# A transformer block on one Trainium2 core: the second half's eight normalised token tiles are turned on VectorE and through DRAM instead of on TensorE, and some background work is moved

## The chip, the cores and the metric

The kernel runs on one core of one Trainium2 chip. The core has four compute engines with queues of their own: PE (TensorE, matmuls), DVE (VectorE), ACT (ScalarE) and POOL (GpSimd), and SP (SyncE), which here only issues DMAs. Each queue is worked off in order. The metric is device microseconds of one execution; lower is better.

## The reference, cut to what matters

2048 tokens of width 576, all float32. The layer norm of x feeds two branches whose results are added to x:

```python
x  = A_x                                          # 1 x 2048 x 576
xn = (x - mean(x)) / sqrt(var(x) + 1e-5)
qkv = xn @ wqkv                                   # 576 x 1728; 32 heads of 18
# query s sees keys s, s-2, ..., s-14 (W = 8, dilation 2; places before 0 masked)
o   = softmax(q . k / sqrt(18)) . v
a   = o @ wo                                      # 576 x 576
h   = xn @ w1 + b1                                # 576 -> 4608
m   = (h * tanh(softplus(h))) @ w2                # Mish; 4608 -> 576
return x + a + m
```

## The kernel before, in words

**Tiling.** The tokens are worked on in two halves of 1024 (`hf` = 0, 1), each half as eight tiles of 128 tokens, four to a block `b` (0, 1). A float32 product is made of three matmul passes on fp32r values: every operand is split into a high part (a cast to fp32r, on ACT) and a low part (operand minus high part, a subtract on DVE or POOL). TensorE contracts over the partitions, so the normalised tokens must lie with the 576 features on the partitions: `XTs[hf, b]` holds them as four 128-feature slices plus a rest of 64, high parts and low parts, 512 tokens wide (the tile `xt_1_0` or `xt_1_1` for the second half).

**How the second half's tokens got there.** `x_load` (L105) fetches a tile of 128 tokens (`xn`), `norm1` (L139) normalises it on ACT, and POOL copies the last 64 features beside themselves (L140). `ln_transpose` copies a rest for block 1 on POOL (L192, L194) and calls `transpose_split`, which turns the tile by five matmuls against an identity (L75, L76), or six where a rest goes with it (L78), into PSUM; ACT casts the high parts out of PSUM (L81, L86) and DVE subtracts the low parts (L82, L87). Each of the eight tiles has a slot `("t", 1, b, jj)` of its own in the plan. Tiles 0 to 2 are turned between the last pieces of the first half's MLP; the other five between the second half's first qkv items.

**The MLP.** A unit `q` makes 256 hidden columns: `m1_part` runs 512-wide matmuls into PSUM banks `h` (L674, L680), `take` copies a bank (L708), DVE adds another bank (`c`, L719), ACT applies Mish (L720) and casts the high part (L725), POOL makes the low part (L726). `m2_pair` then multiplies by w2 in chunks `("p", 0, q, b, p)` of 24 matmuls of 288 columns (L774) into the four PSUM buffers `out`, and DVE adds each result to an accumulator (L778), four adds to a chunk. `q` = 17 is the last unit of the first half; its chunks come in the order (1,0), (1,1), (0,0), (0,1). In the second half most units go through a scheme of seven products to a pair of units: `u_sum` (L808), `u_high` (ACT) and `u_low` (L820) make the left operands, `p_item` multiplies (L866) and adds (L872) or copies (L870) into `accP` tiles, `p_join` (L875, POOL) joins those at the end, and `a_split` (L829) makes the plain operands of the units that follow (multiplied at L887). `y_store` (L1048) sends the first half's accumulators to DRAM.

**Attention** runs beside all this: POOL multiplies (L537, L575), DVE reduces (L542, L581), and each finished pair of heads is turned on DVE (`o_turn`, L597: a 32 x 32 block transpose of 128 x 576) and sent to DRAM by four DMAs of 72 KB (`o_send`, L606), whose access pattern completes the transpose.

**What sets the order.** `plan` is a list of slots; each has its main work and a list of background functions, put there by `before(slot, fn)`. The program is emitted slot by slot, and each engine's queue has its instructions in exactly that order. A slot is one piece of the PE's work (a chunk of 24 matmuls, a part of a unit, a qkv item), or empty. `soon` holds functions for the start of the next slot, `behind_adds` names slots whose attention sum is emitted at the slot's end. Every DMA signals one of eight completion semaphores (DMAHW0 to DMAHW7, called lanes below), taken in turn, and its queue first waits until the DMA that used that lane before has landed.

Of the kernel before, what the change touches and what calls it, by code (L numbers as in the profile page):

```python
# [8 lines left out]
F32 = mybir.dt.float32  # L9
# [8 lines left out]
P = 128  # L18
NH = 2
SH = S // NH  # L20
NB = 2
# [18 lines left out]
def block_kernel(ctx: ExitStack, tc: tile.TileContext, x, wq, wo, w1, b1, w2, mask, out):  # L40
# [26 lines left out]
    def transpose_split(src, dst, col, extra=None, pair=False):  # L67
        n = next(tpn)
        if pair:
            ta, tb = (ps.tile([P, 512], F32, tag="out", bufs=4, name=f"tt{k}_{n}") for k in range(2))  # L70
        else:
            ta = ps.tile([P, 512], F32, tag="h", bufs=4, name=f"ta_{n}")
            tb = ps.tile([P, 512], F32, tag="h", bufs=4, name=f"tb_{n}")
# [29 lines left out]
    def x_load(n):  # L103
        xn = sb.tile([P, 5 * P], F32, tag="xn", bufs=XNB, name=f"xn_1_{n}_{next(tpn)}")
        nc.sync.dma_start(xn[:, 0:D], x_tile(1, n))  # L105
        xns[1, n] = xn
# [30 lines left out]
    def norm1(n):  # L137
        xn = xns[1, n]
        nc.scalar.activation(xn[:, 0:D], xn[:, 0:D], AF.Identity, bias=nm1[:, n, :], scale=rs1[:, n, :])  # L139
        nc.gpsimd.tensor_copy(xn[:, D:D + 64], xn[:, KT * P:D])  # L140

    group = {}
# [41 lines left out]
    def ln_transpose(hf, b, jj):  # L184
# [10 lines left out]
        transpose_split(xn, XTs[hf, b], jj * P, rem if b else None, (hf, b) == (1, 0) and jj < 3)  # L195
# [314 lines left out]
    behind_adds, now = set(), [0]  # L510

    def attention(hf):
# [4 lines left out]
        def flush():  # L517
            if behind[0] is not None:
                if now[0] in behind_adds:
                    tail.append(behind[0])  # L520
                else:
                    behind[0]()
                behind[0] = None

        for pair in range(NQ * UQ // PU):
# [44 lines left out]
            for k, vt in enumerate(vs):  # L570
                for h in range(2):
# [8 lines left out]
                    def red(pr=pr, og=og, c0=k * CU + h * DH, last=(k, h) == (PU - 1, 1), pair=pair):  # L580
                        nc.vector.tensor_reduce(og[:, c0:c0 + DH, :].rearrange("p d j -> p j d"), pr, axis=AX,  # L581
                                                op=ALU.add)
                        if last:
                            soon.append(lambda: o_turn(hf, pair, og))
# [585 lines left out]
    def pr_(hf, q, b, p, alias=None):  # L1170
        def end():
            if hf == 0 and q == NP - 1:
                for jj in (2 * p, 2 * p + 1):
                    y_store(b * JB + jj)
        add(("p", hf, q, b, p), lambda: ((m2_cols if hf else m2_pair)(hf, q, b, p), end()), alias=alias)
# [56 lines left out]
    def tr(b, jj):  # L1232
        add(("t", 1, b, jj), lambda: ln_transpose(1, b, jj))
# [185 lines left out]
    for g, (e, k, s) in enumerate(items):  # L1419
        lead = items[g - 3][2] if g >= 3 else spot(1, 0, 5) + 2 * g  # L1420
        before(lead + 1, lambda e=e, k=k: p_fetch(e, k))
        for qq in range(2):
            ds = {(0, 0): (-6, -5, -5), (0, 1): (-2, -1, 0), (1, 0): (0, -4, -2), (1, 1): (0, -2, -2), (2, 0): (0, -3, -2), (2, 1): (0, -3, -2), (3, 0): (-4, -3, -2), (3, 1): (-4, -2, -1), (4, 0): (0, -3, -3), (4, 1): (0, -3, -2), (5, 0): (-1, -3, -3), (5, 1): (0, -3, -2), (6, 0): (-4, -3, -1), (6, 1): (-4, -3, -2)}[k, qq]
            if (e, k, qq) == (0, 0, 1):
                ds = (-2, -1, -1)
            if (e, k, qq) == (OC - 1, 0, 0):
                ds = (-5, -4, -4)
            for d, f in zip(ds[1:], (u_high, u_low)):
# [3 lines left out]
    J = 2 * OC + 1  # L1432
    for n, (a, b) in enumerate((("P6", "P1"), ("P7", "P6"), ("P6", "P5"), ("P2", "P1"), ("P3", "P6"), ("P4", "P7"), ("P5", "P7"))):
# [3 lines left out]
    for b in range(NB):  # L1437
        for j in range(2):
            before(spot(1, J, 0) + (2,3,1,2)[2 * b + j], lambda b=b, j=j: a_split(b, j))

# [32 lines left out]
    i = spot(0, NP - 2, 0)  # L1473
    for jj in range(JB):
        before(i + 2 * jj, lambda jj=jj: x_load(jj))
        before(i + 2 * jj + 6, lambda jj=jj: norm1(jj))
        before(at["t", 1, 0, jj] + 2, lambda jj=jj: x_load(JB + jj))
    for jj in range(JB):
        before(at["p", 0, NP - 1, 1, 1] + jj, lambda jj=jj: norm1(JB + jj))
# [6 lines left out]

    att = {}
    behind_adds.add((at["p", "x", OC - 1, 4]))
# [123 lines left out]
```

## Time and profile before

| | |
|---|---|
| time, median of 3 runs | 1113.11 us (1113.07 to 1113.46) |
| the profiled execution | 1113.54 us, span 1111.8 us, TensorE clock 1.000 |
| busy, share of the span | PE 99%, DVE 76%, ACT 45%, POOL 71% |
| DMA | 271.6 MB, mean 244 GB/s |

A row of the timeline reads: start in us from the span's start, time from its first start to its last end, engine, line, operation, out<-in, shape, and how many instructions in a row it stands for; in brackets the engine's idle time ahead of it and what ended it. PE matmuls overlap one another, so the time from one row's start to the next row's start, and not the duration, is what a row costs. A group row has the count, the total busy time and the mean duration of one.

### The profile page before, as it was taken

What the parts mean: (1) busy time and instruction counts of PE and PEld (TensorE: products, weight loads), DVE (VectorE), ACT (ScalarE), POOL (GpSimd) and SP (SyncE); (2) the same over time, 40 slices, a digit from 0 to 9 for tenths busy, and PEclk for the clock granted to TensorE, in tenths of its full rate; (3) what the DMA queues carried; (4) which work ended last, traced back from release to release, by engine and by line L of the source; (5) the groups of instructions that cost most, each with busy time, mean ns of one, the idle gap of its engine ahead of it and who ended that gap; (6) DMA issues with size and microseconds to landing.
All of it is one profiled execution on the core that took longest, in us unless ns stands there. A gap on an engine that the chain in (4) does not pass through costs nothing.

```text
span 1111.8 us, 18206 instructions
## 1 busy us (share of the span) xinstructions
PE 1103.0 (99%) x6550; PEld 1014.7 (91%) x6550; DVE 850.0 (76%) x1367; ACT 499.2 (45%) x917; POOL 790.6 (71%) x639
## 2 busy tenths in 40 slices
PE   8999999999999999999999999999999999999998
PEld 8999899999999999999999888989989999999998
DVE  6359788888889888897656577786876677777786
ACT  5544655544454544555333354433433344343353
POOL 2479777766679688685788667666688976867542
PEclk9999999999999999999999999999999999999999
DMA  6899696868777758675598798665674657776674
GB/s 202 283 312 313 229 347 223 283 235 275 259 243 264 266 210 300 248 253 202 188 328 257 228 378 297 217 198 197 222 223 169 210 195 216 244 286 220 181 232 141
DMA packets 178270, 271.60 MB, mean 244 GB/s; under 512 B 53218, under 2 KB 120068, under 8 KB 178180
## 3 DMA queue, kind: packets, MB, share of 16 engines
q1 hardware_dynamic: 178180, 270.44, 71.6%
q8 instruction: 52, 0.85, 0.3%
q14 instruction: 38, 0.31, 0.1%
HBM read 160.39 MB, written 110.00 MB: 243 GB/s over the span
## 4 chain that ended last, share of the span: by engine, by line
PE 86%; POOL 5%; DVE 4%; issue 2%; ACT 2%; DMA 2%; SPq 0%; POOLq 0%; DVEq 0%; ACTq 0%
PE h L674 27%; PE po L774 21%; PE po L887 11%; PE pq L348 9%; PE h L680 5%; PE o L1070 5%; PE po L866 4%; PE z L446 3%; POOL pv L575 1%; POOL s L624 1%; DMA accP<-in_x 1%; POOL accP L875 1%; DVE rm L808 1%; DVE accP L872 0%; DVE u L820 0%
## 5 line engine op out<-in xcount | busy, mean ns | idle before, releaser
L774 PEld LDWEIGHTS po<-w,act 128*128 128x128 f32 x1728 | 236.4, 188 | 6.0 <-POOL act L726 0.4
L774 PE MATMUL po<-w,act 128*128 128x288 f32 x1728 | 240.7, 295 | 0.2 <-POOL act L726 0.2
L537 POOL TENSOR_TENSOR pr<-q,kv 128x576 f32<-128x576 f32 x128 | 197.2, 1566 | 8.0 <-DMA q<-q_d 4.9
L726 POOL TENSOR_TENSOR act<-c,act 128x512 fp32r<-128x512 f32 x81 | 107.4, 1326 | 128.3 <-ACT act L725 128.3
L575 POOL TENSOR_TENSOR pv<-L,kv 128x576 f32<-128x576 f32 x128 | 177.8, 1484 | 26.2 <-DVE L L568 21.2
L778 DVE TENSOR_TENSOR acc<-po,acc 128x288 f32<-128x288 f32 x288 | 119.5, 449 | 29.9 <-PE po L774 28.8
L348 PE MATMUL pq<-wq,xt 128*128 128x432 f32 x672 | 136.4, 361 | 1.0 <-ACT xt L81 1.0
L887 PEld LDWEIGHTS po<-w,act 128*128 128x128 f32 x960 | 130.8, 188 | 4.5 <-POOL act L829 1.2
L887 PE MATMUL po<-w,act 128*128 128x288 f32 x960 | 133.4, 295 | 1.0 <-POOL act L829 1.0
L348 PEld LDWEIGHTS pq<-wq,xt 128*128 128x128 f32 x672 | 125.0, 188 | 8.0 <-ACT xt L81 1.6
L720 ACT ACTIVATE c<-c,b1c 128x512 f32<-128x512 f32 x81 | 58.7, 725 | 140.5 <-DVE c L719 140.3
L674 PE MATMUL h<-xt,t 128*128 128x512 f32 x432 | 110.6, 391 | 0.2 <-DVE c L719 0.2
L674 PE MATMUL h<-S,t 128*128 128x512 f32 x432 | 110.7, 391 | 0.0
L542 DVE TENSOR_REDUCE L<-pr 128x64 f32<-128x1152 f32 x64 | 85.8, 1342 | 26.3 <-POOL pr L537 26.2
L581 DVE TENSOR_REDUCE og<-pv 128x144 f32<-128x1152 f32 x64 | 86.0, 1346 | 25.7 <-POOL pv L575 25.6
L674 PE MATMUL h<-xt,wa 128*128 128x512 f32 x432 | 104.1, 390 | 0.0
L708 ACT COPY c<-h 128x512 f32<-128x512 f32 x81 | 47.4, 586 | 124.8 <-PE h L680 73.8
L866 PEld LDWEIGHTS po<-pw,u 128*128 128x128 f32 x672 | 92.0, 188 | 5.3 <-issue 0.9
L674 PEld LDWEIGHTS h<-xt,wa 128*128 128x128 f32 x432 | 80.9, 188 | 17.0
L866 PE MATMUL po<-pw,u 128*128 128x288 f32 x672 | 94.7, 296 | 1.3 <-issue 0.5
L674 PEld LDWEIGHTS h<-xt,t 128*128 128x128 f32 x432 | 79.1, 188 | 15.2 <-DVE c L719 0.5
L890 DVE TENSOR_TENSOR accP<-po,accP 128x288 f32<-128x288 f32 x160 | 68.8, 453 | 29.1 <-PE po L887 27.5
(228 smaller groups left out, 1854.2 us busy)
## 6 DMA issues: line engine op xcount, KB each, us to landing
kv<-kv_d SPq DMA_DIRECT2D x64, 396.0 KB, 5.0
kept_t<-t SPq DMA_DIRECT2D x36, 512.0 KB, 4.6
t<-kept_t SPq DMA_DIRECT2D x36, 512.0 KB, 6.4
rw<-in_w SPq DMA_DIRECT2D x36, 320.0 KB, 4.6
kept_wa<-wa SPq DMA_DIRECT2D x18, 640.0 KB, 4.7
kept_w<-w SPq DMA_DIRECT2D x20, 576.0 KB, 3.7
wa<-kept_wa SPq DMA_DIRECT2D x18, 640.0 KB, 4.8
w<-kept_w SPq DMA_DIRECT2D x20, 576.0 KB, 4.2
```

What stands on the lines that cost most here:

```text
L348: nc.tensor.matmul(pq[:, 0:432], XT[:, xi, tok], wt[wi][:, hl, 0:432], start=i == 0, stop=i == len(seq) - 1)
L537: nc.gpsimd.tensor_tensor(out=pr[:, x:x + hh], in0=q[:, j0 + x:j0 + x + hh, None, :].to_broadcast([P, hh, W, CU]), in1=win(kt, 0, CU, j0 + ...
L542: nc.vector.tensor_reduce(L[:, k, j0:j0 + hj].rearrange("p j w h -> p (j w h)"), pr.rearrange("p j w (h d) -> p (j w h) d", h=2), axis=AX, ...
L575: nc.gpsimd.tensor_tensor(out=pr[:, x:x + hj].rearrange("p j d w -> p j w d"), in0=L[:, k, x:x + hj, :, h:h + 1].to_broadcast([P, hj, W, DH]),
L581: nc.vector.tensor_reduce(og[:, c0:c0 + DH, :].rearrange("p d j -> p j d"), pr, axis=AX, op=ALU.add)
L674: nc.tensor.matmul(ph, wt[:, wl, wk * P:(wk + 1) * P], X[:, xs, :], start=first and i == 0, stop=last and i == len(seq) - 1, skip_group_ch ...
L726: nc.gpsimd.tensor_tensor(out=a[:, 1, :], in0=t, in1=a[:, 0, :].bitcast(F32), op=ALU.subtract)
L774: nc.tensor.matmul(po, acts[hf, q, b, j][:, al, tok], done["w2", hf, 2 * q + j][:, wl, c * HC:(c + 1) * HC], start=i == 0, stop=i == 5)
L778: nc.vector.tensor_tensor(out=t, in0=po, in1=t, op=ALU.add)
L866: nc.tensor.matmul(po, units[e, k, qq][:, al, tok], w[:, qq, wl, :], start=i == 0, stop=i == 5)
L887: nc.tensor.matmul(po, acts[hf, q, b, j][:, al, tok], done["w2", hf, 2 * q + j][:, wl, c * HC:(c + 1) * HC], start=i == 0, stop=i == 5)
L890: nc.vector.tensor_tensor(out=t, in0=po, in1=t, op=ALU.add)
```

## The change

For the second half only, the turn of the eight tiles leaves TensorE.

- **Taken out:** `ln_transpose(1, ...)`, that is 44 matmuls of 128 x 128 (four tiles of five, four of six), their PSUM tiles, the ACT casts and DVE subtracts that read these, and POOL's eight copies at L140. The slots `("t", 1, b, jj)` stay, empty.
- **Put in, per tile:** the load, now 3 or 6 slots before the turn (in a `raw` buffer for tiles 4 to 7), `norm1` one slot before the turn, `x_turn` (after's L143, a DVE block transpose of 128 x 576 into `xT_a` or `xT_b` in turns), `x_put` (L152: four DMAs of 72 KB, issued on ACT's queue, one in each of the four slots after the turn, to a DRAM tile `xT_d`), `x_back` (L156, L159: three DMAs on SP's queue, 256 KB and two of 32 KB, into an `xn` buffer, features now on the partitions), `x_high` (the casts on ACT, L180, and POOL's rest, as before) and one slot later `x_low` (the subtracts on DVE, L185), both now reading SBUF.
- **When:** with e the slot `("t", 1, 0, 3)`, which stands ahead of the first half's last chunks, the turns are at e-22, e-19, e-16, e-13, e-9, e-6, e-3 and e; the casts at e, e+2, e+4, e+6 (block 0) and e+7, e+9, e+11, e+13 (block 1).
- **Moved beside that:** `a_split` goes ahead of the `p_join`s of its slot; the low part of the operand S3's second unit (`u_low`, k = 0) comes one slot earlier for every pair of units; for the first pair, two sums come at other slots; three attention pieces are emitted later in or after their slot (`behind_adds`, `behind_next`, `o_turn`); `y_store` comes two slots after its chunk instead of at the chunk's end.

```diff
+    def x_turn(n):
+        if n == 0:
+            xTs["a"] = sb.tile([P, D], F32, tag="acc", bufs=9, name="xT_a")
+            xTs["b"] = sb.tile([P, 2 * 432], F32, tag="r3", bufs=1, name="xT_b")[:, 0:D]
+        t = xTs["ab"[n % 2]]
+        nc.vector.transpose(t, xns[1, n][:, 0:D])
+        xTs[n] = t
+
+    def x_put(n, g):
+        t = xTs[n]
+        if g == 0:
+            xT_d[n] = dram.tile([D, P], F32, name=f"xT_d{n}")
+        rows = xT_d[n].rearrange("(n i) p -> i n p", i=32)
+        part = slice(g * 32, (g + 1) * 32)
+        nc.scalar.dma_start(rows[:, :, part], t[part].rearrange("i (n k) -> i n k", k=32))
+
+    def x_back(n):
+        xn = xns[1, n] = sb.tile([P, 5 * P], F32, tag="xn", bufs=XNB, name=f"xn_t_{n}")
+        nc.sync.dma_start(xn[:, 0:KT * P].rearrange("p (k t) -> p k t", k=KT),
+                          xT_d[n][0:KT * P].rearrange("(k p) t -> p k t", p=P))
+        for r_ in range(2):
+            nc.sync.dma_start(xn[r_ * 64:(r_ + 1) * 64, KT * P:], xT_d[n][KT * P:D])
...
+    def x_high(n):
...
+        if b == 0:
+            nc.gpsimd.tensor_copy(rem, xr)
+        else:
+            nc.gpsimd.tensor_tensor(out=rem, in0=rem, in1=xr, op=ALU.subtract)
+        for s_, hi, lo in x_parts(n):
+            nc.scalar.copy(hi, s_)
+
+    def x_low(n):
+        for k, (s_, hi, lo) in enumerate(x_parts(n)):
+            r_ = slice(64 if k else 0, P)
+            nc.vector.tensor_tensor(out=lo[r_], in0=s_[r_], in1=hi[r_].bitcast(F32), op=ALU.subtract)
...
-        add(("t", 1, b, jj), lambda: ln_transpose(1, b, jj))
+        add(("t", 1, b, jj))
...
+    i, e = spot(0, NP - 3, 8), at["t", 1, 0, JB - 1]
+    for n in range(TJ):
+        b_, jj = divmod(n, JB)
+        turn = e - 9 + 3 * jj if b_ else i + 3 * jj + 3
+        split = e + (7, 9, 11, 13)[jj] if b_ else e + 2 * jj
+        before(turn - (6 if b_ else 3), lambda n=n: x_load(n, "raw" if n >= JB else "xn"))
+        before(turn - 1, lambda n=n: norm1(n))
+        before(turn, lambda n=n: x_turn(n))
+        for g in range(4):
+            before(turn + 1 + g, lambda n=n, g=g: x_put(n, g))
+        before(e + 2 + 2 * jj if b_ else split - 6, lambda n=n: x_back(n))
+        before(split, lambda n=n: x_high(n))
+        before(split + 1, lambda n=n: x_low(n))
...
-    behind_adds.add((at["p", "x", OC - 1, 4]))
+    behind_adds.update((at["p", "x", OC - 1, 4], at["p", "x", 0, 4]))
+    behind_next.add(at["m", 1, 10, 3])
```

Three places in the queues. First DVE's queue at e, before. `c21` is the last `c` add of `q` = 17; `tt0`, `tt1`, `ta` and `tb` are PSUM tiles with turned tokens; the first row after the gap is an attention sum, and the adds to `acc_0_1_0` take the results of chunk (1,0):

```order
L82 TENSOR_TENSOR xt_1_0_6052<-tt0_50_6129,xt_1_0_6052 128x4x128
L87 TENSOR_TENSOR xt_1_0_6052<-tt1_50_6130,xt_1_0_6052 64x128
L719 TENSOR_TENSOR c21_0_17_6008<-h3_0_17_5954,c21_0_17_6008 128x512
...
L581 TENSOR_REDUCE og_0_5_6120<-pv_0_5_0_0_6121 128x8x18
L82 TENSOR_TENSOR xt_1_0_6052<-tt0_52_6198,xt_1_0_6052 128x4x128
L87 TENSOR_TENSOR xt_1_0_6052<-tt1_52_6199,xt_1_0_6052 64x128
L82 TENSOR_TENSOR xt_1_0_6052<-ta_54_6227,xt_1_0_6052 128x4x128
L87 TENSOR_TENSOR xt_1_0_6052<-tb_54_6228,xt_1_0_6052 64x128
L778 TENSOR_TENSOR acc_0_1_0_183<-po_0_17_1_0_0_6240,acc_0_1_0_183 128x288
L778 TENSOR_TENSOR acc_0_1_0_183<-po_0_17_1_0_1_6248,acc_0_1_0_183 128x288
```

and in the changed kernel (`xT_a`, `xT_b`: the turned tiles 6 and 7 on their way to DRAM; `xn_t_0`: tile 0 come back):

```order
L143 STREAM_TRANSPOSE xT_a_5679<-xn_1_6_50_6047 128x576
L771 TENSOR_TENSOR c21_0_17_6034<-h3_0_17_5979,c21_0_17_6034 128x512
...
L629 TENSOR_REDUCE og_0_5_6149<-pv_0_5_0_0_6150 128x8x18
L143 STREAM_TRANSPOSE xT_b_5680<-xn_1_7_51_6102 128x576
L185 TENSOR_TENSOR xt_1_0_6240<-xn_t_0_6096,xt_1_0_6240 128x4x128
L185 TENSOR_TENSOR xt_1_0_6240<-xn_t_0_6096,xt_1_0_6240 64x128
L830 TENSOR_TENSOR acc_0_1_0_183<-po_0_17_1_0_0_6262,acc_0_1_0_183 128x288
L830 TENSOR_TENSOR acc_0_1_0_183<-po_0_17_1_0_1_6270,acc_0_1_0_183 128x288
```

The two subtracts ahead of the `c21` add have become the turn of tile 6; the four ahead of chunk (1,0)'s adds have become the turn of tile 7 and the low parts of tile 0.

Second, ACT's queue at the same place, before (the first two rows finish the `c22` operand, and the rows of L720 and L725 in the middle the `c21` operand of chunk (1,0)):

```order
L720 ACTIVATE c22_0_17_6074<-c22_0_17_6074,b1c_122 128x512
L725 CAST act_0_1_35_6080<-c22_0_17_6074 128x512
L81 CAST xt_1_0_6052<-tt0_50_6129 128x4x128
L86 CAST xt_1_0_6052<-tt1_50_6130 128x128
L720 ACTIVATE c21_0_17_6008<-c21_0_17_6008,b1c_122 128x512
L725 CAST act_0_1_34_6154<-c21_0_17_6008 128x512
L81 CAST xt_1_0_6052<-tt0_52_6198 128x4x128
L86 CAST xt_1_0_6052<-tt1_52_6199 128x128
```

and in the changed kernel, with the semaphores that each row waits for (DMAHW: a lane; `xT_d_6144` is tile 5 in DRAM, `xn_6` tile 6 under `norm1`):

```order
L772 ACTIVATE c_0_17_6094<-c_0_17_6094,b1c 128x512 [waits DVE_49]
L777 CAST act_1_35_6106<-c_0_17_6094 128x512 [waits Activation_49,Pool_49]
L152 DMA xT_d_6082<-xT_a 32x18x32 [waits DMAHW7_49]
L152 DMA xT_d_6144<-xT_b 32x18x32 [waits DMAHW1_49]
L152 DMA xT_d_6144<-xT_b 32x18x32 [waits DMAHW3_49]
L136 ACTIVATE xn_6_50_6047<-xn_6_50_6047,nm_107,rs_104 128x576 [waits DMAHW6_49]
L152 DMA xT_d_6144<-xT_b 32x18x32 [waits DMAHW5_49]
L772 ACTIVATE c_0_17_6034<-c_0_17_6034,b1c 128x512 [waits DVE_49]
L777 CAST act_1_34_6177<-c_0_17_6034 128x512 [waits Activation_49]
L152 DMA xT_d_6144<-xT_b 32x18x32 [waits DMAHW6_49]
```

The casts from PSUM are gone from between the two operands; in their place stand four puts and the normalising of tile 6. By the order of the lanes the second put of tile 5 (lane 3) waits for the landing of `q_0_12` (an attention load, L500, on SP's queue), the first put of tile 6 (lane 0) for `q_0_13`, and the second put of tile 6 (lane 2) for the first DMA of tile 3's `x_back`, which itself (lane 3) waits for the second put of tile 5.

Third, POOL's queue where the products are joined, before (the `act` rows are the low parts that `a_split` makes for the units after the last pair, the `pr` row is an attention multiply):

```order
L537 TENSOR_TENSOR pr_1_3_0_0_9172<-q_1_6_8854,kv0_1_6_8852 128x576 x2
L875 TENSOR_TENSOR accP6_0_7863<-accP6_0_7863,accP1_0_7480 128x576
L875 TENSOR_TENSOR accP6_1_7880<-accP6_1_7880,accP1_1_7659 128x576
L829 TENSOR_TENSOR act_1_1_16_9259<-rm2_7261,act_1_1_16_9259 128x512
L875 TENSOR_TENSOR accP7_0_7531<-accP7_0_7531,accP6_0_7863 128x576
L875 TENSOR_TENSOR accP7_1_7548<-accP7_1_7548,accP6_1_7880 128x576
L829 TENSOR_TENSOR act_1_0_16_9284<-ra2_7257,act_1_0_16_9284 128x512
L829 TENSOR_TENSOR act_1_1_17_9287<-rt0_7264,act_1_1_17_9287 128x512
```

and in the changed kernel:

```order
L585 TENSOR_TENSOR pr_1_3_0_0_9194<-q_1_6_8876,kv0_1_6_8874 128x576 x2
L881 TENSOR_TENSOR act_1_1_16_9279<-rm2_7283,act_1_1_16_9279 128x512
L927 TENSOR_TENSOR accP6_0_7885<-accP6_0_7885,accP1_0_7502 128x576
L927 TENSOR_TENSOR accP6_1_7902<-accP6_1_7902,accP1_1_7680 128x576
L881 TENSOR_TENSOR act_1_0_16_9304<-ra2_7279,act_1_0_16_9304 128x512
L881 TENSOR_TENSOR act_1_1_17_9307<-rt0_7286,act_1_1_17_9307 128x512
L927 TENSOR_TENSOR accP7_0_7551<-accP7_0_7551,accP6_0_7885 128x576
L927 TENSOR_TENSOR accP7_1_7568<-accP7_1_7568,accP6_1_7902 128x576
```

The low part `act_1_1_16` now comes ahead of the first two joins, and `act_1_0_16` and `act_1_1_17` ahead of the next two.

More of the change, by code (lines that the diff above doesn't have):

```diff
@@ L1170, in pr_ @@
     def pr_(hf, q, b, p, alias=None):
[L1171 to L1175, printed above, removed]
+        add(("p", hf, q, b, p), lambda: (m2_cols if hf else m2_pair)(hf, q, b, p), alias=alias)
     items = []
```

63 lines of the change are left out of this document (37 added, 26 removed).

## The prediction

> **What bounds the kernel now.** I read the busy shares first, then PE's timeline wherever a gap stands between its rows, then the other engines' rows there.
>
> ```profile
> PE 1103.0 (99%) x6550; PEld 1014.7 (91%) x6550; DVE 850.0 (76%) x1367; ACT 499.2 (45%) x917; POOL 790.6 (71%) x639
> 477.00:501.00 24.00, 24.00 (x147) 22.01 (x147) 22.00 (x31) 12.40 (x20) 21.03 (x19) 1.00 0.69 241
> ```
>
> PE is busy for 99% of the span, so only two things can pay: matmuls that go away, and the few stalls in PE's row. The second line (a window: length, then busy time of PE, weight loads, DVE, ACT, POOL, then clock and DMA share) is the stretch into which the first three turns come. There DVE has 2.0 us left in 24, ACT 11.6.
>
> The sum is made against the profiled execution's own 1113.54 us; the median of the runs is 0.43 lower, which is taken off at the end. Less than 0.2% (2.2 us) can't be told from no change here.
>
> **Taken out: 44 transposes on PE.** PE's timeline, without and with them:
>
> ```profile
> 508.60 1.53 PE L674 MATMUL h<-S,t 128*128 128x512 f32 x6
> 509.97 3.34 PE L774 MATMUL po<-w,act 128*128 128x288 f32 x24
> 513.15 0.60 PE L75 MATMUL tt<-ident,xn 128*128 128x128 f32 x4
> ...
> 515.08 0.62 PE L680 MATMUL h<-xt,wc 128*128 128x512 f32 x2
> ...
> 541.72 0.76 PE L348 MATMUL pq<-wq,xt 128*128 128x432 f32 x3
> 542.31 3.35 PE L774 MATMUL po<-w,act 128*128 128x288 f32 x24
> 545.50 0.60 PE L75 MATMUL ta<-ident,xn 128*128 128x128 f32 x4
> ...
> 548.92 0.60 PE L75 MATMUL ta<-ident,xn 128*128 128x128 f32 x4
> ```
>
> Start to start counts, since durations overlap. Six 512-wide matmuls alone take 509.97 - 508.60 = 1.37 us; five transposes and six such matmuls take 515.08 - 513.15 = 1.93. So five cost 0.56. Six transposes with fourteen 432-wide matmuls take 548.92 - 545.50 = 3.42, the fourteen at (542.31 - 541.72) / 3 = 0.197 each 2.75: six cost 0.67. Four tiles of each: 4 x (0.56 + 0.67) = 4.92 us off PE, all on the path. The rows' steps of 0.01 to 0.02 us leave 0.2 of doubt in that. 1113.54 - 4.92 = 1108.62.
>
> **The moves beside it: seven stalls of PE.** The rows on either side of each (in brackets idle time and what ended it):
>
> ```profile
> 658.81 0.61 PE L674 MATMUL h<-xt,t 128*128 128x512 f32 x2
> 659.60 2.68 PE L866 MATMUL po<-pw,u 128*128 128x288 f32 x15 [0.17 <-ACT accP L870]
> ...
> 686.47 0.61 PE L680 MATMUL h<-xt,wc 128*128 128x512 f32 x2
> 687.24 1.98 PE L866 MATMUL po<-pw,u 128*128 128x288 f32 x13 [0.16 <-DVE accP L872]
> ...
> 746.92 2.24 PE L866 MATMUL po<-pw,u 128*128 128x288 f32 x13
> ...
> 792.36 0.82 PE L866 MATMUL po<-pw,u 128*128 128x288 f32 x5
> 793.34 1.89 PE L866 MATMUL po<-pw,u 128*128 128x288 f32 x12 [0.16 <-DVE u L820]
> ...
> 827.94 0.81 PE L887 MATMUL po<-w,act 128*128 128x288 f32 x5
> 829.71 1.99 PE L887 MATMUL po<-w,act 128*128 128x288 f32 x13 [0.96 <-POOL act L829]
> ...
> 864.31 0.96 PE L887 MATMUL po<-w,act 128*128 128x288 f32 x6
> 865.50 1.65 PE L674 MATMUL h<-xt,t 128*128 128x512 f32 x6 [0.23 <-DVE c L719]
> ```
>
> Undisturbed, a 288-wide matmul takes (513.15 - 509.97) / 24 = 0.1325 us and a 512-wide one 0.228. What is over that is the stall: at 659.60, 0.79 - 0.46 = 0.33; inside its fifteen matmuls 2.68 - (1.98 + 2 x 0.1325) = 0.43; at 687.24 0.31; inside 746.92's thirteen 2.24 - 1.98 = 0.26; at 793.34 0.98 - 0.66 = 0.32; at 829.71 1.77 - 0.66 = 1.11; at 865.50 1.19 - 0.80 = 0.39. Together 3.15 us.
>
> Every one of them gets a move: 829.71 the split ahead of the joins, 687.24 the attention sum behind the `accP` adds, 865.50 the attention sum behind the `c` add, 746.92 and 793.34 the low part a slot earlier, 659.60 the first pair's sums. The largest can be followed on POOL:
>
> ```profile
> 823.10 1.29 POOL L829 TENSOR_TENSOR act<-rm,act 128x512 fp32r<-128x512 f32 x1
> 824.36 2.82 POOL L875 TENSOR_TENSOR accP<-accP,accP 128x576 f32<-128x576 f32 x2
> 827.13 1.30 POOL L829 TENSOR_TENSOR act<-ra,act 128x512 fp32r<-128x512 f32 x1
> ```
>
> Two joins stand between the split of 823.10 and the two from 827.13 on; behind those instead, the splits come 2.8 us sooner against a stall of 1.1, and the joins feed only later joins and adds. The other stalls are 0.3 to 0.4, the instructions moved out of the way 0.8 to 1.3 us long. Ends: 3.15, and half of it, 1.6, if what is put back makes its own consumer late. I take 3.15, because each move is several times its stall. 1108.62 - 3.15 = 1105.47.
>
> **Put in: the turns.** The nearest rows, the first half's attention doing the same kind of thing:
>
> ```profile
> L597 DVE STREAM_TRANSPOSE oT<-og x16: 762/778/781, 140.9 to 1049.1; 128x576 f32<-128x576 f32 x16
> L606 SPq DMA_DIRECT2D o_d<-oT x72: 303/507/1700, 142.9 to 1053.7; - x72
> o_d<-oT SPq DMA_DIRECT2D x64, 72.0 KB, 2.4
> o<-o_d SPq DMA_DIRECT2D x16, 320.0 KB, 5.4
> q<-q_d SPq DMA_DIRECT2D x32, 144.0 KB, 5.7
> L139 ACT ACTIVATE xn<-xn,nm,rs x8: 862/866/880, 491.6 to 537.8; 128x576 f32<-128x576 f32 x8
> L82 DVE TENSOR_TENSOR xt<-ta,xt 128x512 fp32r<-128x512 f32 x13 | 9.0, 690 | 11.6 <-ACT xt L81 11.5
> L255 DVE TENSOR_TENSOR t<-tt,t 128x512 fp32r<-128x512 f32 x36 | 45.1, 1253 | 3.9 <-ACT t L254 3.9
> ```
>
> Durations are in ns, DMA landings (last figure) in us. DVE gets 8 turns of 0.78 us, and its 8 large subtracts now read two SBUF operands: 1.25 as in the L255 row instead of 0.69, at the worst. ACT gets 32 issues of 0.5 us, 16 us; its casts stay. SP gets 24 issues of `x_back`, 12 us; POOL loses eight copies. DMA gets 8 x 2 x 288 KB more. Nearly all of it runs beside PE. Where it can reach PE:
>
> *First, the stretch of 477 to 501.* DVE's 22.01 us plus three turns, 2.34, make 24.35 in 24.0: 0.35 too much, so PE waits about 0.4 us for adds there. Ends: 0, and 2.3 if no idle time takes any of it.
>
> *Second, the first half's last two chunks, at e.*
>
> ```profile
> 516.29 0.44 SPq L500 DMA_DIRECT2D q<-q_d  x1
> 522.47 0.72 ACT L720 ACTIVATE c<-c,b1c 128x512 f32<-128x512 f32 x1 [2.35 <-DVE c L719]
> 523.23 0.62 ACT L725 CAST act<-c 128x512 fp32r<-128x512 f32 x1
> 523.93 1.29 POOL L726 TENSOR_TENSOR act<-c,act 128x512 fp32r<-128x512 f32 x1 [0.39 <-ACT act L725]
> 527.16 6.61 PE L774 MATMUL po<-w,act 128*128 128x288 f32 x48
> 529.80 1.55 DVE L778 TENSOR_TENSOR acc<-po,acc 128x288 f32<-128x288 f32 x4
> ...
> xn<-in_x SPq DMA_DIRECT2D x16, 288.0 KB, 4.8
> ...
> xn<-in_x SPq DMA_DIRECT2D x4, 288.0 KB, 3.9
> ```
>
> Four turns of five gone, PE is at chunk (1,0) 2.2 us sooner, 525.0, or 525.4 with the 0.4 above. Its operand is now made behind ACT's puts. The second put of tile 5 waits for the lane of `q_0_12`; that load, issued at 516.29 before, goes out 1.1 us sooner (two turns gone), at 515.2, and lands by the row's 5.7 at 520.9. Then one issue 0.5, the normalising of tile 6 0.87, its turn on DVE 0.78, the `c` add behind it 0.69, Mish and cast 1.34, POOL 1.29: 526.4, so PE waits 1.0. Queued behind that put on ACT are the normalising, Mish and the cast; behind the turn on DVE the `c` add; behind both, PE.
>
> Chunk (1,1) starts 24 x 0.1325 = 3.2 us later and needs PSUM that DVE's adds at 529.80 free. Ahead of those now stand the turn of tile 7 and the low parts of tile 0; tile 7 is normalised behind the second put of tile 6, whose lane is the first DMA of tile 3's `x_back`, whose lane is the second put of tile 5. From 520.9: put 0.5 and landing 2.4, `x_back` 0.5 and 5.4, put 0.5, normalising 0.87, turn 0.78, low parts about 1.5, an add 0.39: 533.7, where PE stands ready at 530.3 - 2.2 + 0.4 + 1.0 = 529.5. That is 4.2 more, 5.2 for both chunks.
>
> The landings in that sum are medians of the whole run. In the stretch around e (505 to 535, the last row) the token loads land in 3.9 instead of 4.8, a fifth less. With 4.6 and 4.4 for the two long landings and 0.69 for the low part the first wait is nil, the second 2.6. And with the fastest landings both go to nothing. Ends 0 and 5.2; I take 2.9, near the value that this stretch's own rows give. 1105.47 + 0.4 + 2.9 = 1108.77, less 0.43: **1108.3 us.**
>
> The rest costs PE nothing: the casts of tiles 1 to 7 come two slots apart, with qkv items from e+3 on; `x_back`s now stand ahead of the weights `wq` on SP, covered by the two chunks still to run (6.6 us at 527.16). If that cover is too short, the first qkv item waits for what is over.
>
> [...]
>
> **Rivals.**
>
> *The waits at e are hidden.* The puts' lanes clear before ACT comes to them, since every DMA in question was issued slots before. For it: the window's landings are shorter than the medians, and 72 KB land in 2.4. Against it: the chain above is in the program's order, and ACT can't pass a waiting put. Time: 1108.3 - 2.9 = 1105.4.
>
> *The waits eat the lead and the repairs hold by half.* Landings as the medians: +2.3; stalls that move on to the next consumer: +1.6. For it: DVE has no room at 477 to 501. Time 1112.2, within 0.2% of no change.
>
> *Slower: the puts' ring.* `x_turn` of tile n waits until all four puts of tile n-2 have landed. The last put goes out four slots after its turn, the turn that waits for it comes six slots after; 22 slots from the first turn (about 482.5) to e take 44.7 us, so two slots are 4.1 us. A put that lands within 4.1 us costs nothing.
>
> ```profile
> DMA to landing us min/median/max: 1.8/2.7/8.5
> ```
>
> That is the row of all transfers to and from `o_d`. If the puts landed in 8.5, each lap of two tiles would slip 4.4, three laps 13.2, of which 2.9 are in the sum: 1108.3 + 10.3 = 1118.6. It decides for slower (over 1115.3) from a landing of 7.4 us. Against it: the median of puts of this very shape is 2.4.
>
> [...]
>
> **How the numbers follow.** The forecast's case 0.52 (1108.3, with its own range 1106.5 to 1110.8), hidden waits 0.24 (1105.4), lost lead 0.14 (1112.2), the ring 0.10 (1118.6). Faster than 1110.9 are the first two, 0.76; within 0.2% the third, 0.14; slower the fourth, 0.10. The range leaves out the ring and the outer half of the third: 1104.5 to 1112.2.
>
> **What would show it.** No matmul against the identity after the first half's; PE's rows at 659, 687, 747, 793, 829 and 865 (some 3 us sooner) without a gap; ACT's issues of `xT_d` with a wait for a DMA at tiles 5 and 6; PE's idle time ahead of chunks (1,0) and (1,1) of `q` = 17 at 0 to 1 and 2 to 4 us. Wrong would make it: puts that land later than 4 us; qkv items that wait for a cast, which means that `x_back` is the late step; a `wq` weight late on SP; or a new gap behind one of the moved sums.

## The result, and the profile after

The changed kernel takes 1125.87 us (median of 4 runs, 1124.83 to 1127.30) against 1113.28 for the kernel before (4 runs): a ratio of 1.0114 (95% interval 1.0101 to 1.0126), 12.6 us slower where 4.8 faster was forecast. The profiled execution took 1124.83, 11.3 more than the one shown of before. DVE, ACT and POOL do about what they did. PE is busy less and stands more; the list of what it waited for (us in total, times, longest) begins so:

```profile
PE po L826 <- DVE acc L830: 5.4, 2, 4.3
PE h L726 <- DVE c L771: 2.4, 1, 2.4
PE po L939 <- DVE accP L942: 2.4, 2, 1.7
...
PE pq L394 <- DMA wq<-kept_wq: 1.2, 4, 0.7
PE z L492 <- DVE zqs L505: 0.9, 1, 0.9
PE po L826 <- POOL act L778: 0.8, 1, 0.8
```

The first two and the last are the last chunks of the first half's MLP, where the turns run. PE's timeline there:

```profile
515.40 3.35 PE L826 MATMUL po<-w,act 128*128 128x288 f32 x24
521.13 1.66 PE L726 MATMUL h<-xt,t 128*128 128x512 f32 x6 [2.39 <-DVE c L771]
...
527.65 0.62 PE L732 MATMUL h<-xt,wc 128*128 128x512 f32 x2
529.40 0.53 PE L826 MATMUL po<-w,act 128*128 128x288 f32 x2 [1.13 <-DVE acc L830]
530.75 3.18 PE L826 MATMUL po<-w,act 128*128 128x288 f32 x22 [0.83 <-POOL act L778]
538.20 6.06 PE L826 MATMUL po<-w,act 128*128 128x288 f32 x24 [4.27 <-DVE acc L830]
544.10 2.12 PE L394 MATMUL pq<-wq,xt 128*128 128x432 f32 x10
```

At PE's pace before (0.1325 us to a 288-wide matmul, 0.228 to a 512-wide one) the starts come late by 521.13 - 515.40 - 3.18 = 2.5 us, then 1.75 - 0.46 = 1.3 at 529.40, 1.35 - 0.27 = 1.1 at 530.75 and 7.45 - 2.92 = 4.5 at 538.20. With 0.6 at 506 (not shown) that is 10.0 us of waiting. And chunk (1,1) itself takes 544.10 - 538.20 = 5.90 us where 24 matmuls take 3.18: 2.7 us more. The windows say why (length, busy time of PE, weight loads, DVE, ACT, POOL, then the granted clock and the DMA share; the first line is of before, the others of after; the last is the stretch at half clock, read off the trace's record of the clock):

```profile
520.00:530.00 10.00, 10.00 (x69) 9.39 (x68) 7.42 (x15) 5.29 (x11) 8.75 (x12) 1.00 0.64 222
```

```profile
520.00:530.00 10.00, 7.66 (x42) 6.40 (x42) 7.55 (x16) 4.48 (x6) 4.42 (x4) 1.00 1.06 306
537.23:544.06 6.83, 5.86 (x24) 5.86 (x25) 4.48 (x10) 1.45 (x4) 6.09 (x7) 0.50 0.79 201
```

The clock granted to PE fell to half (0.50) while it stood for 4.3 us, and stayed there for the whole of chunk (1,1); and the DMA engines, which had room before (0.64), are full (1.06).

What held PE is written in the queues of ACT, SP and DVE. ACT, DVE and SP in the changed kernel (times of issue for the DMAs):

```profile
522.93 1.98 ACTq L152 DMA_DIRECT2D xT_d<-xT_b  x2
524.95 0.87 ACT L136 ACTIVATE xn<-xn,nm,rs 128x576 f32<-128x576 f32 x1 [2.40 <-DMA q<-q_d]
...
531.97 3.06 ACTq L152 DMA_DIRECT2D xT_d<-xT_a  x2
535.08 0.87 ACT L136 ACTIVATE xn<-xn,nm,rs 128x576 f32<-128x576 f32 x1 [5.74 <-DMA xn_t<-xT_d]
```

```profile
526.59 0.78 DVE L143 STREAM_TRANSPOSE xT_a<-xn 128x576 f32<-128x576 f32 x1 [2.38 <-DMA xn_t<-xT_d]
527.29 0.65 DVE L771 TENSOR_TENSOR c<-h,c 128x512 f32<-128x512 f32 x1
...
535.98 0.78 DVE L143 STREAM_TRANSPOSE xT_b<-xn 128x576 f32<-128x576 f32 x1 [5.33 <-ACT xn L136]
536.68 0.97 DVE L185 TENSOR_TENSOR xt<-xn_t,xt 128x512 fp32r<-128x512 f32 x2
537.68 1.55 DVE L830 TENSOR_TENSOR acc<-po,acc 128x288 f32<-128x288 f32 x4
```

```profile
519.49 0.79 SPq L546 DMA_DIRECT2D q<-q_d  x1
...
529.22 0.43 SPq L156 DMA_DIRECT2D xn_t<-xT_d  x1
```

Tile 6 is normalised at 524.95, after ACT has stood 2.40 us on the second put of tile 5, whose lane `q_0_12` held; `q_0_12`, issued at 519.49, had landed some 5 us later. Its turn on DVE came at 526.59, another 0.8 us after the end of the normalising (525.82): the buffer was free only when the last put of tile 4, issued at 521.95, had landed at 526.46 (the row names a take-back; by the trace's landings it was this put). Tile 7 is normalised at 535.08, after 5.74 us on the second put of tile 6, whose lane the take-back of tile 3 held; that was issued at 529.22. Behind each stands the turn on DVE, and behind the turn the add for which PE waits.

### The profile page after: what moved, and what is told of

Read it like the earlier page. It is cut to its first block, busy times and chain, and to the rows that moved or that the text cites. A ratio compares the mean times of both kernels' runs of the same rounds, so it can differ in the third digit from the quotient of the medians.

```text
span 1123.0 us, 18208 instructions
## 1 busy us (share of the span) xinstructions
PE 1101.3 (98%) x6506; PEld 1011.3 (90%) x6506; DVE 861.5 (77%) x1379; ACT 498.9 (44%) x921; POOL 789.1 (70%) x631
## 4 chain that ended last, share of the span: by engine, by line
PE 82%; DMA 6%; DVE 4%; POOL 4%; ACT 2%; issue 1%; SPq 1%; ACTq 0%; DVEq 0%; POOLq 0%
PE h L726 25%; PE po L826 17%; PE po L939 11%; PE pq L394 11%; PE po L918 6%; PE o L1122 5%; PE h L732 5%; PE z L492 3%; DMA xn_t<-xT_d 1%; POOL pv L623 1%; POOL act L778 1%; DMA accP<-in_x 1%; DMA kept_wa<-wa 1%; DMA wq<-kept_wq 1%; DMA t<-kept_t 1%
```

## The experiments

All are measured against the kernel before on the same chip; where a ratio is given, the interval is 95%.

**1. The side moves alone (`side_only`).** The kernel before with every move beside the turn:

```diff
-            ds = {(0, 0): (-6, -5, -5), (0, 1): (-2, -1, 0), ...
+            ds = {(0, 0): (-6, -5, -5), (0, 1): (-2, -1, -1), ...
+            if e == 0 and k in (3, 5):
+                ds = (-3, -2, -1) if k == 3 else (1,) + ds[1:]
...
+    ... (in words: the two loops of a_split now stand ahead of the loop of p_join)
-    behind_adds.add((at["p", "x", OC - 1, 4]))
+    behind_adds.update((at["p", "x", OC - 1, 4], at["p", "x", 0, 4]))
+    behind_next.add(at["m", 1, 10, 3])
```

Not shown are the moves of `o_turn` and `y_store` and the lines that `behind_next` needs; they are in the run as in the change.

> The kernel before with all of the change's side moves (splits ahead of joins, sums, attention pieces, y_store) and the tokens still turned on PE. Theory one, the prediction's: the seven stalls of PE at 659 to 865 us go and nothing comes for them, 3.15 us less than before, 1110.1. Theory two, from the profile after: there the rows at 829 and 865 are clean, but PE waits 0.7 us at 701 (DVE rt behind an attention sum) and 2.4 us at 845 (DVE accP behind joins on POOL) in their place; if those waits belong to the moves and not to the later turn, the moves bring nothing: 1113.3 to 1114.

Measured: 1112.6 us, ratio 0.9985 (0.9976 to 0.9995). A gain, but about half of the 3.15 us summed for it. PE's rows at the two places that were expected to be dear:

```profile
689.57 1.65 PE L680 MATMUL h<-xt,t 128*128 128x512 f32 x6 [0.71 <-DVE rt L725]
...
833.82 1.85 PE L893 MATMUL po<-w,act 128*128 128x288 f32 x12 [1.66 <-DVE accP L896]
836.39 1.86 PE L893 MATMUL po<-w,act 128*128 128x288 f32 x12 [0.73 <-DVE accP L896]
```

The stall of 1.1 us at 830 is gone, and 4 us later PE waits 2.4 us for adds. What DVE waits for there:

```profile
832.04 1.35 DVE L544 TENSOR_REDUCE L<-pr 128x64 f32<-128x1152 f32 x1 [7.11 <-POOL pr L539]
833.32 0.81 DVE L896 TENSOR_TENSOR accP<-po,accP 128x288 f32<-128x288 f32 x2
835.88 0.82 DVE L896 TENSOR_TENSOR accP<-po,accP 128x288 f32<-128x288 f32 x2 [1.75 <-POOL accP L881]
```

An attention sum that waits for POOL stands ahead of the adds, and the next adds wait for a join that POOL now makes after a split. POOL has the same work as before; what PE no longer waits for first, it waits for next.

**2. The turn alone (`turn_only`).** The changed kernel with all of those moves undone.

> The changed kernel with the side moves undone: the turn through DRAM alone. If the side moves gain 3.15 us wherever they stand, this one is that much slower than the changed kernel, 1129. If they only move stalls about, it is within 1 us of the changed kernel's 1125.9. In both cases the waits of about 10 us at 506 to 538 us and the half clock after them stay.

Measured: 1127.33 us, ratio 1.0114 (1.0099 to 1.0130), the same ratio as the whole change. So beside the turn the side moves are worth nothing that these runs can tell, and the turn alone makes the loss. In its profile PE stood 3.6 us for the accumulators' adds, 3.5 for `c`, and 4.3 at the z stage. The half clock came twice there (from 520.89 and from 537.96, 6.83 us each), the first time in a stall of 3.2 us that ended at 522.

**3. The puts on SP's queue (`puts_sp`).**

```diff
-        nc.scalar.dma_start(rows[:, :, part], t[part].rearrange("i (n k) -> i n k", k=32))
+        nc.sync.dma_start(rows[:, :, part], t[part].rearrange("i (n k) -> i n k", k=32))
```

> The changed kernel with the 32 puts issued from SP's queue instead of ACT's. Theory one: the waits come from ACT's queue standing behind lanes that SP's transfers hold, with normalising, Mish and casts queued behind them; then they fall from 10 us to under 3, the clock stays at 1.0, and the time is about 1115. Theory two: the landing of the puts themselves (4.8 us median here, 2.4 for the first half's) is what the turns wait for, from whichever queue; then the waits stay over 7 us and the time over 1122.

Measured: 1117.46 us, ratio 1.0032 (1.0020 to 1.0043). Two thirds of the loss are gone with one word: most of it needs the puts to stand in ACT's queue. But the waits, by the rows' starts, fell to 4.6 us and not under 3. What is left is on DVE:

```profile
523.16 0.78 DVE L143 STREAM_TRANSPOSE xT_a<-xn 128x576 f32<-128x576 f32 x1 [2.24 <-DMA xT_d<-xT_b]
...
530.10 0.78 DVE L143 STREAM_TRANSPOSE xT_b<-xn 128x576 f32<-128x576 f32 x1 [2.87 <-DMA xT_d<-xT_b]
```

Now the turns themselves wait for puts to land, those of the tile two before, since there are two buffers. (The first row names the other buffer; by the trace's landings it was the last put of tile 4 that landed at 523.1, just before this turn, and the last of tile 5 at 530.0 before the second.) The clock stayed at 1.0.

**4. A third buffer, puts on ACT (`act_three`).**

```diff
+        if n % 3 == 2:
+            xTs["c"] = sb.tile([P, 5 * P], F32, tag="xn", bufs=XNB, name=f"xT_c_{n}")[:, 0:D]
-        t = xTs["ab"[n % 2]]
+        t = xTs["abc"[n % 3]]
```

> The changed kernel, puts on ACT's queue as in it, with three buffers for turned tiles in place of two. Theory one, lanes: ACT's puts still wait for the loads and take-backs that hold their lanes, so normalising, Mish and casts still come late; PE's waits at 506 to 540 stay over 6 us and the time over 1121. Theory two, the two buffers: turns waited for the landing of puts two tiles before; the waits at 506 to 540 fall under 3 us.

Measured: 1117.71 us, ratio 1.0035 (1.0021 to 1.0049). Neither theory had it: the waits at 506 to 540 are 4.7 us by the rows' starts, between the two. The largest left is one of 2.2 us:

```profile
528.59 0.53 PE L828 MATMUL po<-w,act 128*128 128x288 f32 x2 [2.18 <-DVE acc L832]
```

It is still a wait of the first kind: tile 6 is normalised at 524.87, after ACT has stood 3.8 us for puts. In this profiled execution, the slowest of the four, the clock then fell to half from 529.75 to 533.16, which cost 1.5 us more. So each of the two, ACT's queue and the two buffers, is needed for the full loss; taking away either leaves under half of the waits.

**5. Both (`puts_sp_three`).**

> The changed kernel with the puts on SP's queue and three buffers for turned tiles in place of two, so that a turn waits for the puts of the tile three before. With two buffers and the puts on SP, DVE stood 2.2 and 2.9 us before the turns of tiles 6 and 7 for the landing of puts, and PE 4.4 us at 526 to 533. If the two buffers are what is left of the ring, PE's waits there fall under 1.5 us and the time to about 1114. If the transfers of this stretch are too slow in any case (DMA share 1.0), the waits stay over 3 us.

Measured: 1119.97 us, ratio 1.0059 (1.0045 to 1.0073), slower than with two buffers, though the waits for the turns are gone altogether:

```profile
524.67 6.53 PE L828 MATMUL po<-w,act 128*128 128x288 f32 x48
531.03 1.34 PE L396 MATMUL pq<-wq,xt 128*128 128x432 f32 x6
534.88 1.45 PE L396 MATMUL pq<-wq,xt 128*128 128x432 f32 x6 [2.50 <-DMA wq<-kept_wq]
537.67 1.06 PE L396 MATMUL pq<-wq,xt 128*128 128x432 f32 x2 [1.34 <-DMA wq<-kept_wq]
```

The 48 matmuls of both chunks run through at the pace of before, 2.5 us earlier than there. Then the first qkv items wait for weights, which SP issues between puts and take-backs, and the clock falls to half again after it (fifteen 288-wide matmuls from 538.53 on take 3.80 us; the mean granted clock of this execution is 0.997). With neither the puts in ACT's queue nor the two buffers, the waits before the two chunks are gone, so the two together made them; the full DMA engines alone did not, for their share over 505 to 535 is 0.97 here as in the changed kernel. The gain was passed on to the next transfer. Whether SP's order or the full DMA engines make the weights late was not taken apart. (The third buffer is one of `xn`'s; what that took from the token loads was not measured by itself.)

**6. The 44 transposes left out (`no_transposes`).** The kernel before; the casts and subtracts read the normalised tile from SBUF.

```diff
+        if pair is None:
+            sav = src[:, 0:KT * P].rearrange("p (k t) -> p k t", k=KT)
+            nc.scalar.copy(hi, sav)
+            nc.vector.tensor_sub(dst[:, 5:5 + KT, col:col + P], sav, hi.bitcast(F32))
...
+            return
```

> The kernel before with the 44 transposes of the second half left out: the casts and subtracts read the normalised tokens as they lie, so the second half is computed from tokens that are not turned. This prices what leaves PE and nothing else. By the rows' starts 4.9 us less than before, 1108.4; by the durations (44 x 272 ns) 12.0 less, 1101.3.

Measured: 1114.17 us, ratio 1.0002 (0.9993 to 1.0012). Neither: even without a put or a take-back, the transposes' absence brings nothing, give or take 1 us. The stand-in is not quite free: its subtracts on DVE read two SBUF operands, and the one ahead of the adds that chunk (1,1) needs took 1.61 us where the one from PSUM took 0.69. PE waits 1.0 us there. With the side moves of experiment 7 the same question was asked again:

> The kernel before without the second half's transposes (its second half is computed from tokens that are not turned), with the side moves of side_best. Without transposes alone PE's 4.9 us came back as a wait of 2.1 at the z stage (593), a lower clock after it and 1.2 at 532. If the z stage is the limit, a new wait of 2 us or more stands there and the ratio to before is that of side_best alone, 0.997. If the turn of the attention output moved to the next slot frees it, the 4.9 come on top: ratio 0.992 to 0.993.

Measured: 1112.87 us, ratio 0.9996 (0.9987 to 1.0005). Of the 4.9 us 1.6 are gone again at the last two chunks, behind the stand-in's subtracts. The rest goes at the z stage, where PE and ACT stand like this:

```profile
588.27 0.36 PE L456 MATMUL z<-zxn_T,xt 128*128 128x432 f32 x1
590.89 1.45 PE L456 MATMUL z<-z_T,S 128*128 128x432 f32 x3 [2.26 <-ACT zqs L465]
592.13 1.28 PE L456 MATMUL z<-zmn_T,S 128*128 128x432 f32 x3
```

```profile
589.74 0.62 ACT L670 CAST S<-s 128x512 fp32r<-128x512 f32 x1 [4.30 <-POOL s L638]
...
590.55 0.28 ACT L465 COPY zqs<-z 128x144 f32<-128x144 f32 x1
```

PE needs PSUM that ACT's copies free; these stand behind a cast that has waited 4.30 us for a sum on POOL. POOL alternates there between those sums and attention's multiplies without a gap. In the kernel before PE came just late enough: at 590.86 ACT's copies stood 1.3 us for PE, and at 595 PE waited 0.3. Coming 3.4 us sooner, PE waits 2.4 us and then runs at half clock (0.50 from 591 to 593): the eight matmuls from 590.89 to 593.93 take 3.0 us instead of 1.6. In all 3.9 us, which is the lead and a little more.

**7. The side moves less two (`side_best`).** Without the splits ahead of the joins and without the attention pieces behind the adds.

> The kernel before with the side moves less two: without the splits ahead of the joins, and without the attention pieces put behind the adds. In the run with all side moves and no turn PE stood 1.8 and 0.9 us at 834 and 836 (accP adds behind joins) and 0.9 at 690 (rt behind the attention sum), where the kernel before stands 1.1 at 830 and 0.3 at 687. If those two moves make those waits, this run saves 1.6 and 0.9 us against all side moves: about 3.5 us less than before, a ratio of 0.997. If the waits come from the other moves, they are still there and the ratio is 0.9985.

Measured: 1112.48 us, ratio 0.9995 (0.9986 to 1.0003). A miss: not better than all the moves. The waits at 834 and 836 are gone, and the one at 829 is back as before, 0.9 us; but at 686 PE waits 1.7 us for adds behind a sum of the first pair of units and an attention sum, where with all the moves it waited 0.2. So the first pair's sums need the attention sum moved with them.

**8. The z stage relieved (`no_transposes_z`).** Without transposes, with the moves of experiment 9, and

```diff
+        geng[0] = nc.vector if (hf, c) == (1, 1) and k in (1, 2) else nc.gpsimd
...
-        nc.gpsimd.tensor_tensor(out=o, in0=f(a), in1=f(b), op=op)
+        geng[0].tensor_tensor(out=o, in0=f(a), in1=f(b), op=op)
```

> The kernel before without the second half's transposes (computed from tokens that are not turned), with the side moves of side_pick, and with two of the z stage's sums (the last 256 columns, second and third sum) on DVE in place of POOL. Theory one: the 4.9 us that PE saves are lost at the z stage because ACT's copies there stand behind a cast that waits for POOL's sums; then with POOL relieved the wait of 2.3 us and the half clock after it at 589 to 593 go, and the ratio is that of side_pick less 0.003 to 0.004. Theory two: the z stage waits for something else (attention, DMA); then the wait stays and the ratio is that of side_pick.

Measured: 1112.84 us, ratio 0.9987 (0.9978 to 0.9996). The wait at the z stage fell from 2.3 to 1.2 us and the clock held there (the eight matmuls from 589.84 to 591.51 take 1.7 us), which is the direction of theory one. But 0.35 us came at the next step, and at 828 PE waits 1.8 us with half clock after it (0.998 in the mean of this execution). That wait does not come from the z stage: `side_pick` has it too (1.9 us, without the half clock: 1.000 in the mean), behind its split on DVE. From the z stage to there PE was 0.5 to 0.9 us ahead of `side_pick`, not 4.9. In time it is no better than the side moves alone: what is saved at one stage is waited for at the next. Theory one is shown for the wait, not for the time.

**9. One split on DVE instead (`side_pick`).**

```diff
-        nc.gpsimd.tensor_tensor(out=a[:, 1, :], in0=t, in1=a[:, 0, :].bitcast(F32), op=ALU.subtract)
+        (nc.vector if (b, j) == (1, 1) else nc.gpsimd).tensor_tensor(
+            out=a[:, 1, :], in0=t, in1=a[:, 0, :].bitcast(F32), op=ALU.subtract)
```

> The kernel before with all side moves except the splits ahead of the joins; in place of that, the low part of the last but one split (act_1_1_17, for which PE stands 1.1 us at 830) is made on DVE, which is idle there from 826 to 832. If the joins made late by the splits are what cost 1.8 and 0.9 us at 834 in the run with all side moves, those waits go and PE has no wait over 0.4 there: about 2.7 us less than that run, 1110, ratio to before 0.996 to 0.997. If the wait for accP adds stays, it has another cause and the ratio is 0.9985 or more.

Measured: 1112.23 us, ratio 0.9990 (0.9982 to 0.9999). A miss: the split stands ahead of adds on DVE and waits 4.2 us for its cast, and PE waits 1.9 us at 829 for those adds. In time it can't be told from the side moves as they were (0.9985); both are just faster than the kernel before, by 0.10 and 0.15%.

**10. PE made to stand (`gap6`, `gap3`).** The kernel before with six, or three, turns on DVE ahead of the adds that free PSUM for chunk (1,1); their result isn't used.

```diff
+    def busy():
+        t = sb.tile([P, D], F32, tag="acc", bufs=9, name="scratch")
+        for _ in range(6):
+            nc.vector.transpose(t, xns[1, 3][:, 0:D])
+    before(at["p", 0, NP - 1, 1, 0], busy)
```

> The kernel before with six idle turns of a tile (DVE, 0.78 us each) ahead of the adds of the first half's chunk (1,0), which only delay: PE stands about 4.6 us before chunk (1,1), as it stood 4.3 in the changed kernel. If standing alone halves the clock, the 24 matmuls after it take 5.5 to 6 us and not 3.2, and the run is 7 us longer than before. If the half clock in the changed kernel came from something else (its DMAs), the run is 4.6 longer and the chunk takes 3.2.

> As the run with six idle turns ahead of chunk (1,0)'s adds, with three: PE stands about 2.2 us. With 4.6 us the clock was half for about 5 us after. In two other runs PE stood 2.0 and 2.3 us at the z stage and the clock fell, in two it stood 2.1 and 2.4 elsewhere and it did not. If the length alone decides, the clock here is as in most runs of that length; if it depends on where the idle time falls, the chunk after takes 3.2 us (no drop) or about 5 (drop), and either is possible.

Measured: 1120.02 and 1117.47 us, each a single run, 6.8 and 4.2 over the kernel before. First six turns, then three:

```profile
535.19 5.31 PE L774 MATMUL po<-w,act 128*128 128x288 f32 x24 [4.57 <-DVE acc L778]
540.34 2.93 PE L348 MATMUL pq<-wq,xt 128*128 128x432 f32 x14
...
536.00:539.00 3.00, 3.00 (x15) 3.00 (x14) 2.31 (x4) 0.00 (x0) 0.00 (x0) 0.50 0.85 287
```

```profile
533.14 4.97 PE L774 MATMUL po<-w,act 128*128 128x288 f32 x24 [2.13 <-DVE acc L778]
537.95 2.31 PE L348 MATMUL pq<-wq,xt 128*128 128x432 f32 x11
```

In these two runs standing alone was enough to halve the clock (0.50 from 536 to 539 in `gap6`, 0.57 in the mean from 534 to 538 in `gap3`), without a put or a take-back in the kernel: the 24 matmuls take 5.15 and 4.81 us instead of 3.18, so the stall of 4.6 us cost 2.0 more and the one of 2.1 cost 1.6 more.

## Why the prediction was wrong

The step that made the changed kernel slower is the price of the waits at the last two chunks: the sum had 3.3 us for them and for 477 to 501, and they took 10.0, with 2.7 more of half clock, for which there was no term. Beside it two gains did not hold, the transposes' and the side moves'. One after the other:

**Taken out, 4.92 us "all on the path": a second step that failed.** The price of the transposes was read rightly from the starts. That it would be saved was wrong. Without the transposes, with no put or take-back in their place, the kernel takes 1.0002 of its time (0.9993 to 1.0012). A busy share of 99% says that PE has hardly waited, not that nothing else is just as late: at the z stage the engines that feed PE had 1.3 us to spare at one place and none at the next, and a lead of 5 us is more than they can follow. The rows for this were in the profile of before (POOL busy without a gap around the z stage); the prediction looked at what an earlier PE meets at e and nowhere behind it. In the changed kernel itself PE was late when it came to the z stage; there the 4.9 us do stand in the rows, under larger losses.

**The side moves, 3.15 us: half.** Of the seven stalls six are gone; alone the moves gave 0.15%, 1.7 us. The low end that was stated, 1.6, was the right one, for its reason: what was put back makes its own consumer late, at 690 and 834. With the turn in place nothing of it is left (1.0114 with the moves and without).

**The stretch of 477 to 501, 0.4 us: near in size, by luck.** There DVE was busy for 19.5 us of the 24, not all of it, and PE did not wait. 0.6 us came at 506, for a weight's subtract on DVE, which was busy for 9.35 of the 10 us from 500 to 510.

**The last two chunks, 2.9 us: the mechanism right but for one link, the size wrong.** Put behind `q_0_12`, put behind the take-back, normalising, turn, add came as written, and PE's largest wait is the one before chunk (1,1). It summed to 10.0 us with the 0.6 above, not 3.3. What failed is when SP issues. `q_0_12` went out at 519.49 and not at 515.2: SP had issued nothing from 514.7 to 518.0, behind a token load of 511.03 that took 6.9 us to land, and then waited on the lanes of a put and two take-backs. The first take-back of tile 3 went out at 529.22 and not at about 523.8. The link given for it, that its lane is the second put of tile 5, is wrong: it took lane 2 after the first take-back of tile 2, and that lane was free by 528.53. It stood in SP's queue, which had waited until 525.7 for a `wq` load and until 527.2 for a take-back of tile 1. The two long landings themselves, some 5 us for `q_0_12` and 5.5 for the take-back, were near the medians that the sum's upper end took; of the landings only the puts' was far off, 4.8 us in the median and not 2.4:

```profile
DMA to landing us min/median/max: 1.8/4.8/8.8
```

And the turn of tile 6 was not the first victim: tile 5's was, 2.4 us, behind puts whose lanes `wq` loads held. The longer low part of the sum's upper end, about 1.5 us, did not come: tile 0's took 0.97 us for both, as those from PSUM did.

**What was missing: the half clock, 2.7 us.** No term of the sum and no rival had it. Two more losses had no term either, `wq` weights late by 1.9 us at 574 to 577, which the prediction named as a sign of being wrong, and 1.2 us at the z stage.

**The rival that came nearest is the ring**, slower from landings of 7.4 us on, at a chance of 0.10 and 1118.6 us. It was on the right side, but it asked only for the turns' wait on puts; with the landing measured, 4.8, it alone would have slipped 0.7 us a lap by its own sum. In the changed kernel it shows as the 0.8 us before the turn of tile 6. Experiments 3 to 5 show that the full loss takes this wait and ACT's queue together.

**What the puts took of the DMA engines** stands in the packets (505 to 535 us, first before, then after: packets, MB, share of the 16 engines):

```profile
q1 hardware_dynamic: 2573, 6.51, 64.0%
...
q1 hardware_dynamic: 4978, 7.31, 75.7%
q10 hardware_dynamic: 7716, 0.96, 21.0%
```

The puts are the last line: 21.9% for a MB against 10.4% for the rest, 2.1 times the engines' time for a byte. So the puts, with an eighth of the rest's bytes, took over half of what had been spare there.

**The sum by the rows** of the two profiled executions: -4.9 for the transposes, +10.0 of waits at 506 to 538, +2.7 of clock, +1.9 for `wq` weights at 574 to 577, +1.2 at the z stage; at 660 to 866 3.9 of stalls gone (the seven, and one of 0.7 at 666) and 3.8 come (701, 808, 845, 848). Together +10.8, where 11.3 were measured.

## What to carry to other kernels

Before booking work taken off the busiest engine as time, look at the next places where it meets the others and ask how much sooner they could be ready; leaving the work out without a replacement is a cheap test of the most that a change can bring. Don't put DMA issues whose turn depends on other queues' transfers ahead of compute on an engine that works in order: everything behind them inherits the slowest of those transfers, as tile 7's normalising did here after ACT had stood 5.74 us. And take landing times, and the times at which a shared queue gets to its issues, from a stretch as full as the one the change will make.

## What the runs showed of the hardware

In these runs a stall of PE could cost more than its length: with stalls of 4.3 us (the changed kernel) and 4.6 us (`gap6`) the granted clock was 0.5 for 6.8 us. It fell with one of 1.8 us too (`no_transposes_z` at 828), yet after 2.4 us at 521 in the changed kernel and 2.1 us at 533 in `puts_sp` the next matmuls ran at full pace, at a granted clock of 1.00. So the length alone did not decide at this size.

The record of the clock in the traces says more. The stretch at half clock lasted 6.83 us in the changed kernel (537.23 to 544.06) and, both times, in `turn_only`, and half of that, 3.41, in `act_three` (529.75 to 533.16) and `gap3` (534.33 to 537.75); in `turn_only` the changes lie whole multiples of 3.41 us apart (520.89, 527.72, 537.96, 544.79). Cut into steps of 3.41 us from its own changes, a trace shows how long PE stood within a step (columns as above: first the two steps that share the stall at 521 of the changed kernel, then the step ahead of the fall there, then `gap3`'s step with its stall and the one after it):

```profile
516.75:520.17 3.42, 2.00 (x16) 1.76 (x14) 0.45 (x1) 1.87 (x3) 0.00 (x0) 1.00 0.94 176
520.17:523.58 3.41, 2.45 (x12) 2.10 (x13) 3.34 (x9) 2.10 (x3) 0.95 (x1) 1.00 1.06 369
533.82:537.23 3.41, 0.11 (x1) 0.00 (x0) 1.25 (x2) 2.15 (x4) 0.00 (x0) 1.00 1.09 281
...
530.92:534.33 3.41, 1.28 (x10) 1.19 (x10) 3.31 (x8) 0.00 (x0) 2.00 (x3) 1.00 0.01 5
534.33:537.75 3.42, 3.42 (x16) 3.42 (x16) 2.29 (x4) 0.00 (x0) 0.00 (x0) 0.50 0.94 321
```

The stall of 2.4 us at 521 lies across a boundary, 1.42 us in one step and 0.97 in the next, and the clock stayed at 1.00. That of `gap3`, 2.13 us, lies within one step, and the clock was 0.50 in the next. Of the changed kernel's whole steps at full clock from 15 us on, the one ahead of its fall is that in which PE stood longest, 3.30 us; the next longest is 1.61, and the clock stayed at 1.00 after it. In the kernel before, cut the same way, no step has more than 0.68, and the clock stayed at 1.00. So of these two stalls of some 2 us the one within a step was followed by the half clock, and the one across a boundary was not. This is read from the traces; no run moved a stall against the steps on purpose, and what ties the steps to the program, if anything, was not shown.
